# Summing W's first four units in two halves, with the output weight's second half converted behind W's beginning

## The chip, the cores and the metric

One core of a Trainium2 chip runs the whole program. The metric is the device time in microseconds (us), the median of several runs. Five engines work beside one another, each through its own instructions in program order: TensorE (PE, the matmuls), VectorE (DVE), ScalarE (ACT), GpSimd (POOL) and SyncE (SP, which here only issues loads). They wait for one another by semaphores alone.

## What is computed

The reference chains three layers. The first is a decaying linear attention over 2 batches of 8 heads, 768 positions and 64 columns in blocks. Its output x, 1536 tokens by 512, goes through a gated layer without an activation between its last two weights, and the result goes through a mixture of 8 experts that takes the best expert of each token:

```python
a, b = x @ w1, x @ w2
h = (a * b) @ w3            # w3: 1024 x 1024
y = h @ w_out               # w_out: 1024 x 512
logits = y @ w_gate         # 8 experts; the largest one is taken
```

## The kernel before

Since nothing stands between w3 and w_out, the kernel multiplies weights first: W = w3 @ [w_out, w_out @ w_gate], 1024 by 520. Its last 8 columns give the logits. Three products stand for each fp32 product (mm3, L293 to L297): high part by low part, high by high, low by high, where a high part is a cast to the fast fp32 format and a low part is the rest.

**Stages.** First attention (to about 59 us), then W (to about 108 us), then the gate units and the product with W, then the experts. Attention runs eight iterations, one for each batch and pair of heads. Iteration `it` has two parts. `part1(it)` forms the scores on TensorE (L391), masks them on VectorE into `at` (L400), and sums decayed keys by values (L413, the kv product) into states (L421). `part2(it - 1)` follows it: it multiplies `at` by the values (L439) and queries by states (L453), in two halves, and after each half ScalarE casts the result to `xth` (L462) and VectorE forms the rest `xtl` (L463). The last `part2` stands behind the loop. Decayed keys `kd` for the next iteration come from ScalarE at the end of each iteration (`decay_keys`, L362).

**Chunks and ticks.** In the shadow of all this, weights are converted. w1, w2, w3 and w_out come as 64-bit numbers, in chunks of 512 per partition (512 KB, `Item64`). w_out has two items of four chunks (`wo_it`), w3 four (`w3_it`), and a list fixes the order of all chunks. A tick (`Feed.tick`) takes every chunk under way one stage further and then starts the next one, and ticks are written into the program at fixed places (`TICKS` in attention, `run_bg` elsewhere). The stages of a chunk, a tick each:

1. its start: ScalarE turns the raw data into two parts (L132, into a PSUM bank called raw, and L133);
2. VectorE joins them into an fp32 `t` (the pair L135, L138), which frees the raw bank and the chunk's staging slot;
3. ScalarE casts `t` to the high part (L142), and GpSimd forms the low part (L143).

The w_out chunks go on, two at a time (`u_block`):

4. TensorE transposes two chunks' `t` into two banks (L219), ScalarE copies them to `wt` (L222, a pair of copies);
5. TensorE multiplies `wt` by w_gate (L227), and after the fourth chunk ScalarE copies the result to `up` (L236).

`u_ready` sums `up` (L241) and VectorE puts the eight gate columns behind the item's 512 (L250, L251). `feed.need(item)` ticks until an item is done.

**What sets the order.** Each engine keeps the order of the program. Loads are issued on SP in program order too: `LOADS` says how many chunks are loaded in each iteration beside the next queries, keys (`qk`) and keys, values (`kv`). The first four chunks have a place of their own, the others take four staging slots in turn, so chunk n waits for stage 2 of chunk n - 4. PSUM has seven banks for general use (`bank()`); the bank that came free first, in program order, is the next one given out, and whoever writes to it waits for its last reader.

**W.** Sixteen units, one for each block of 128 rows (`fb`) and half of the columns (256 or 264). A unit sums 24 matmuls over the eight blocks `jb` of w_out's rows (`w_steps`), four of the first item and four of the second; then ScalarE casts the sum to `wxh` (L520), VectorE forms `wxl` (L521), and one or two ticks follow (`NW`). Units go by quarters of w3: four units for each item.

Of the kernel before, what the change touches and what calls it, by code (L numbers as in the profile page):

```python
# [32 lines left out]
NW = (2, 1, 1, 1, 1, 1, 1, 1)  # L33
HOOK = 6
OVER = 7
LOADS = (1, 2, 2, 2, 2, 2, 2, 0)
TICKS = ((0, 0, 0, 0), (0, 0, 0, 1)) + ((1, 0, 0, 1),) * 6 + ((0, 0, 1, 0),)
XBW = 265


# [1 line left out]
def tile_moe_chain(ctx, tc, cap, qk, kv, w12, w3i, woi, wgi, e1i, e2i, c32, c16, zero, out):  # L42
# [8 lines left out]
    def pool(name, bufs=1, **kw):  # L51
        return tc.tile_pool(name=name, bufs=bufs, reuse_waits="tile", **kw)
# [3 lines left out]
    ring = ctx.enter_context(pool("ring"))  # L56
# [7 lines left out]
    def bank():  # L64
        return ps.tile([P, 512], F32, tag="b", name="bank")
# [3 lines left out]
    slots = {"ring": ring}  # L69
# [134 lines left out]
    feed = Feed()  # L204

    def run_bg(n=1):
        for _ in range(n):
            feed.tick()
# [29 lines left out]
    def u_ready(it):  # L238
        u = bank()
        for jb in range(4):  # L240
            nc.tensor.matmul(  # L241
                u[:, jb * NE : (jb + 1) * NE],
                it.up[:, jb * P : (jb + 1) * P],
                gsum,
                start=True,
                stop=True,
            )
        it.us = us = u[:, 0 : 4 * NE].rearrange("p (j e) -> p j e", e=NE)
        uh, ul = it.view(it.hi)[:, :, 512:520], it.view(it.lo)[:, :, 512:520]
        nc.vector.tensor_copy(uh, us)  # L250
        nc.vector.tensor_tensor(ul, us, uh.bitcast(F32), op=ALU.subtract)  # L251

    wo_it = [Item64(woi[j], "ring", "01"[j], 520, u_block) for j in range(2)]
    w3_it = [Item64(w3i[j], "ring", "23"[j]) for j in range(2)]
    w3_it += [Item64(w3i[j], "p0", "w3") for j in range(2, 4)]
    w12_it = [Item64(w12[j], "ring", "2301"[j]) for j in range(4)]
    for n in range(2):
# [7 lines left out]
    for w, e, j in turn[0:2] + turn[4:5] + turn[2:4] + turn[5:]:  # L265
        tag = min(until, key=until.get)
        it = Item((e1i, e2i)[w][e, j], "p3g" if tag == "x" else "ring", tag)
# [26 lines left out]
    def mm3(acc, wh, wl, rh, rl, first, last):  # L294
        nc.tensor.matmul(acc, wh, rl, start=first, stop=False)  # L295
        nc.tensor.matmul(acc, wh, rh, start=False, stop=False)  # L296
        nc.tensor.matmul(acc, wl, rh, start=False, stop=last)  # L297


    with pool("att", 2, side="right") as ap, pool("att1", side="right") as a1:  # L300
# [56 lines left out]
        def decay_keys(it):  # L357
            if it == 8:
                return
            kds[it] = ap.tile([P, NC - 1, P], F32, tag="kd", name="kd", bufs=1)  # L360
            for h in range(2):
                nc.scalar.activation(  # L362
                    kds[it][:, :, h * 64 : h * 64 + 64],
                    loads[it][1][:, 0, 0 : NC - 1, h * 64 : h * 64 + 64],
                    AF.Copy,
                    scale=dmask[:, (it // 2 * 2 + h) % 4, P - 1 : P],
                )
# [63 lines left out]
        def part2(it, ticks, qs, at, st):  # L431
            pair, b = divmod(it, 2)
            tkv = loads[it][1]
            os = [bank(), bank()]
            for cc in range(NC):
                half, c = divmod(cc, 3)
                for h in range(2):
                    hs = slice(h * 64, h * 64 + 64)
                    nc.tensor.matmul(  # L439
                        os[half][hs, c * P : (c + 1) * P],  # L440
                        tkv[:, 1, cc, hs],
                        at[:, h, cc, :],
                        start=c == 0,
                        stop=cc == 0,
                        skip_group_check=True,
                    )
            for half, o in enumerate(os):
                for c in range(3):
                    cc = half * 3 + c
                    for h in range(2):  # L450
                        hs = slice(h * 64, h * 64 + 64)
                        if cc:
                            nc.tensor.matmul(  # L453
                                o[hs, c * P : (c + 1) * P],
                                st[hs, cc - 1, :],
                                qs[hs, cc, :],
                                start=False,
                                stop=True,
                                skip_group_check=True,
                            )  # L460
                xh, xl = xt[2 * b + half]
                nc.scalar.copy(xh[:, pair, :], o[:, 0:G])  # L462
                nc.vector.tensor_tensor(  # L463
                    xl[:, pair, :], o[:, 0:G], xh[:, pair, :].bitcast(F32), op=ALU.subtract
                )
                if half == 0:
                    run_bg(ticks[2])

        prev = None
        for it in range(8):  # L470
            cur = part1(it, TICKS[it])
            if prev is not None:
                part2(it - 1, TICKS[it], *prev)
            if it + 2 < 8:
                load_qkv(it + 2)
            prev = cur
            feed.load(LOADS[it])
            if it == 2:
                nc.scalar.dma_start(wg_sb, wgi)
            if TICKS[it][3]:  # L480
                feed.tick(mid=lambda: decay_keys(it + 1))
# [4 lines left out]
        feed.need(wo_it[0])  # L486
        part2(7, TICKS[8], *prev)
        run_bg(TICKS[8][3])
        feed.auto = True
        feed.need(*wo_it)  # L490
        woh = [it.view(it.hi) for it in wo_it]
        wol = [it.view(it.lo) for it in wo_it]


    wpool = late.enter_context(pool("wext", side="right"))
    wxh = wpool.tile([P, 8, 520], F32R, name="wxh")
    wxl = wpool.tile([P, 8, 520], F32R, name="wxl")
    with pool("p0", 2, side="right") as p0:
        slots["p0"] = p0
        enabled.update(w3_it + w12_it[:2])  # L500
        halves = (slice(0, 256), slice(256, 520))

        def w_steps(acc, fb, cs, jbs):
            item = w3_it[fb // 2]
            fs = slice(fb % 2 * P, (fb % 2 + 1) * P)
            lh = item.hi[:, 0:2048].rearrange("p (j f) -> p j f", f=256)
            ll = item.lo[:, 0:2048].rearrange("p (j f) -> p j f", f=256)
            for jb in jbs:
                mm3(
                    acc,  # L510
                    lh[:, jb, fs],
                    ll[:, jb, fs],
                    woh[jb // 4][:, jb % 4, cs],
                    wol[jb // 4][:, jb % 4, cs],
                    jb == 0,
                    jb == 7,
                )

        def w_out(acc, fb, cs):
            nc.scalar.activation(wxh[:, fb, cs], acc, AF.Copy, scale=2.0**-16)  # L520
            nc.vector.scalar_tensor_tensor(  # L521
                wxl[:, fb, cs],
                acc,
                2.0**-16,
                wxh[:, fb, cs].bitcast(F32),
                op0=ALU.mult,
                op1=ALU.subtract,
            )
            run_bg(NW[fb])

        for i in range(4):
            units = [(fb, cs) for cs in halves for fb in (2 * i, 2 * i + 1)]
            feed.need(w3_it[i])
            for n, (fb, cs) in enumerate(units):
                acc = bank()[:, 0 : cs.stop - cs.start]
                w_steps(acc, fb, cs, range(8))
                if i + n == 0:
                    u_ready(wo_it[1])
                w_out(acc, fb, cs)

    gp = late.enter_context(pool("gt", 9, side="right"))
    p2 = late.enter_context(pool("p2", 2, side="right"))
# [28 lines left out]
    def x2_half(blk, cs, hooks={}):  # L571
        g, tb = divmod(blk, 3)
        ts = slice(tb * P, (tb + 1) * P)
        acc = bank()[:, 0 : cs.stop - cs.start]
        for fb in range(8):
            gh, gl = gts[g, fb]
            mm3(acc, gh[:, ts], gl[:, ts], wxh[:, fb, cs], wxl[:, fb, cs], fb == 0, fb == 7)
            if fb in hooks:
                hooks[fb]()
        return acc  # L580
# [161 lines left out]
    xd, accs = {}, {}  # L742
# [69 lines left out]
    acc = x2_half(NBLK - 1, slice(0, 256), {HOOK: lambda: dispatch(0, 1, apart=True)})  # L812
# [74 lines left out]
    for e in range(NE):  # L887
# [12 lines left out]
        for s in range(nmain):  # L900
            acc = bank()
            ss = slice(s * P, (s + 1) * P)
            for fb in range(8):
                it = e2_it[2 * e + fb // 4]
# [90 lines left out]
```

## Time and profile before

| what | value |
|---|---|
| median of 3 runs | 516.88 us |
| lowest and highest | 516.68 and 518.69 us |
| the profiled execution's own time | 516.84 us |
| its span, first to last instruction | 514.8 us |
| mean granted TensorE clock | 0.997 of full |
| TensorE busy | 498.6 us, 97% |
| VectorE, ScalarE busy | 264.9 and 242.9 us |

Busy times are of one profiled execution. A matmul's row is longer than the distance to the next row, since matmuls are pipelined: the pace is read from the starts. An instruction's idle time is that of its engine just before it, and what ended it is inferred from semaphores; where the engine named had long been done, it was another one.

### The profile page before, as it was taken

The page shows a single profiled execution, that of the slowest core. Times are in us where ns is not written, and L with a number is a line of the kernel's source. Part 1 is how long each engine was busy: PE and PEld are TensorE (multiplying, and loading weights), DVE is VectorE, ACT ScalarE, POOL GpSimd, SP SyncE. Part 2 cuts the span into 40 slices and gives each one's busy share as a digit, 9 for nine tenths or more (in the row PEclk, how much of TensorE's full clock was granted, in tenths as well). Part 3 has the DMA queues.
Part 4 walks back from the last instruction along what each step waited for, and adds up shares of the span by engine and source line. Part 5 has one row for each costly group of instructions (what it writes and reads, how often), then busy time and mean ns, then how long its engine had stood idle before and what let it go on. Part 6 is the DMA issues. An engine that isn't in the chain of part 4 may idle for free. (4 is left out here: it accounts for less than half of the span.)

```text
span 514.8 us, 9557 instructions
## 1 busy us (share of the span) xinstructions
PE 498.6 (97%) x3805; PEld 468.7 (91%) x3805; DVE 264.9 (51%) x576; ACT 242.9 (47%) x485; POOL 128.7 (25%) x124
## 2 busy tenths in 40 slices
PE   8999999999999999999999998899999999999993
PEld 4888999999999999999999998789989898989892
DVE  5998875668332223222332563468383746547420
ACT  2697997789311221122112424457464746546310
POOL 4365664545100000000020005405414040410101
PEclk9999999999999999999999999999999999999998
DMA  8999565557801000100010224486666666574200
GB/s 325 413 410 375 155 227 204 189 187 247 320 26 41 1 0 23 43 1 0 23 43 0 88 69 157 162 299 219 214 213 211 224 224 228 177 250 171 83 2 34
DMA packets 24529, 80.80 MB, mean 157 GB/s; under 512 B 3642, under 2 KB 5692, under 8 KB 24480
## 3 DMA queue, kind: packets, MB, share of 16 engines
q1 hardware_dynamic: 18976, 70.35, 38.4%
q0 software_dynamic: 3344, 7.85, 4.8%
q10 hardware_dynamic: 2160, 1.94, 1.1%
q8 instruction: 32, 0.52, 0.4%
q14 instruction: 17, 0.14, 0.1%
HBM read 74.84 MB, written 10.54 MB: 166 GB/s over the span
## 5 line engine op out<-in xcount | busy, mean ns | idle before, releaser
L97 DVE TENSOR_TENSOR wlo<-st,whi 128x512 fp32r<-128x512 f32 x128 | 82.0, 684 | 16.7 <-ACT whi L95 16.7
L295 PE MATMUL bank<-xtl,whi 128*128 128x384 f32 x256 | 87.1, 340 | 0.0
L297 PE MATMUL bank<-xth,wlo 128*128 128x384 f32 x256 | 86.4, 337 | 0.0
L296 PE MATMUL bank<-xth,whi 128*128 128x384 f32 x256 | 85.8, 335 | 0.0
L95 ACT CAST whi<-st 128x512 fp32r<-128x512 f32 x128 | 73.1, 621 | 16.2 <-PE bank L297 10.7
L787 PE MATMUL bank<-xdl,whi 128*128 128x256 f32 x256 | 72.6, 283 | 4.7 <-issue 2.5
L787 PE MATMUL bank<-xdh,whi 128*128 128x256 f32 x256 | 72.2, 282 | 0.0
L787 PE MATMUL bank<-xdh,wlo 128*128 128x256 f32 x256 | 72.1, 282 | 0.0
L143 POOL TENSOR_TENSOR wlo<-t,whi 128x512 fp32r<-128x512 f32 x40 | 51.9, 1298 | 52.1 <-ACT whi L142 46.5
L295 PE MATMUL bank<-wxl,gh 128*128 128x264 f32 (+1 forms) x192 | 55.9, 291 | 0.0
L296 PE MATMUL bank<-wxh,gh 128*128 128x264 f32 (+1 forms) x192 | 54.1, 282 | 0.0
L297 PE MATMUL bank<-wxh,gl 128*128 128x264 f32 (+1 forms) x192 | 54.1, 282 | 0.0
L787 PEld LDWEIGHTS bank<-xdl,whi 128*128 128x128 f32 x256 | 48.4, 189 | 5.6 <-issue 2.7
L564 DVE TENSOR_TENSOR a_sb<-bank,a_sb 128x384 f32<-128x384 f32 x32 | 17.8, 557 | 66.9 <-PE bank L297 66.3
L295 PE MATMUL bank<-wlo,hh 128*128 128x512 f32 x128 | 51.1, 399 | 0.0
L297 PE MATMUL bank<-whi,hl 128*128 128x512 f32 x128 | 50.4, 394 | 0.0
L718 POOL DMA_INDIRECT out_dram<-y,idx x16 | 16.6, 1038 | 134.2 <-ACT y L920 101.1
L296 PE MATMUL bank<-whi,hh 128*128 128x512 f32 x128 | 50.0, 391 | 0.0
L800 DVE SCALAR_TENSOR_TENSOR hl<-bank,hh 128x512 fp32r<-128x512 f32 x32 | 22.1, 690 | 53.3 <-ACT hh L799 45.5
L787 PEld LDWEIGHTS bank<-xdh,whi 128*128 128x128 f32 x256 | 48.3, 189 | 0.3
L787 PEld LDWEIGHTS bank<-xdh,wlo 128*128 128x128 f32 x256 | 48.4, 189 | 0.0
L295 PEld LDWEIGHTS bank<-xtl,whi 128*128 128x128 f32 x256 | 48.1, 188 | 0.0
(109 smaller groups left out, 1006.1 us busy)
## 6 DMA issues: line engine op xcount, KB each, us to landing
st<-e1i SPq DMA_DIRECT2D x32, 512.0 KB
st<-e2i SPq DMA_DIRECT2D x32, 512.0 KB
st<-w3i SPq DMA_DIRECT2D x16, 512.0 KB
st<-w SPq DMA_DIRECT2D x16, 512.0 KB
tqk<-qk SPq DMA_DIRECT2D x8, 768.0 KB
tkv<-kv SPq DMA_DIRECT2D x8, 768.0 KB
st<-woi SPq DMA_DIRECT2D x8, 512.0 KB
out_dram<-zero SPq DMA_DIRECT2D x1, 3072.0 KB
```

The source lines that it names most:

```text
L95: nc.scalar.copy(h, s)
L97: nc.vector.tensor_tensor(lo, s, h.bitcast(F32), op=ALU.subtract)
L143: nc.gpsimd.tensor_tensor(lo, t, h.bitcast(F32), op=ALU.subtract)
L295: nc.tensor.matmul(acc, wh, rl, start=first, stop=False)
L296: nc.tensor.matmul(acc, wh, rh, start=False, stop=False)
L297: nc.tensor.matmul(acc, wl, rh, start=False, stop=last)
L564: nc.vector.tensor_tensor(a_sb, acc, a_sb, op=ALU.mult)
L718: nc.gpsimd.indirect_dma_start(out=out, out_offset=bass.IndirectOffsetOnAxis(ap=idx[:, col : col + 1], axis=0), in_=src, in_offset=None, b ...
L787: nc.tensor.matmul(o, w[:, k, :], x[:, k, :], start=m == 0 and k == 2 and x is xl, stop=m == 1 and k == 1 and w is lo, skip_group_check=True,)
L800: nc.vector.scalar_tensor_tensor(hl, acc, 0.0, hh.bitcast(F32), op0=ALU.max, op1=ALU.subtract)
```

## The change

The order of items becomes w_out's first, w3's first, w_out's second, w3's second, by building the two lists in turn. Attention has a tick less, in the middle of iteration 3, and its second iteration loads one chunk in place of two. The wait for both w_out items ahead of W is gone. W's first four units are summed over `jb` 0 to 3 one after the other, each into a bank of its own that stays open, with a tick behind each; then `need` asks for w_out's second item, and the four are summed over `jb` 4 to 7 and go out as before. The gate sum of the second item (`u_ready`) stays behind the first finished unit. The other twelve units are as they were. `wt` for chunks that come in W is taken from W's pool.

```diff
--- before.py
+++ after.py
@@ -33,8 +33,9 @@
 NW = (2, 1, 1, 1, 1, 1, 1, 1)
 HOOK = 6
 OVER = 7
-LOADS = (1, 2, 2, 2, 2, 2, 2, 0)
-TICKS = ((0, 0, 0, 0), (0, 0, 0, 1)) + ((1, 0, 0, 1),) * 6 + ((0, 0, 1, 0),)
+LOADS = (1, 1, 2, 2, 2, 2, 2, 0)
+TICKS = ((0, 0, 0, 0), (0, 0, 0, 1), (1, 0, 0, 1), (0, 0, 0, 1)) + ((1, 0, 0, 1),) * 4
+TICKS += ((0, 0, 1, 0),)
 XBW = 265
 
 
@@ -250,8 +251,10 @@
         nc.vector.tensor_copy(uh, us)
         nc.vector.tensor_tensor(ul, us, uh.bitcast(F32), op=ALU.subtract)
 
-    wo_it = [Item64(woi[j], "ring", "01"[j], 520, u_block) for j in range(2)]
-    w3_it = [Item64(w3i[j], "ring", "23"[j]) for j in range(2)]
+    wo_it, w3_it = [], []
+    for j in range(2):
+        wo_it.append(Item64(woi[j], "ring", "01"[j], 520, u_block))
+        w3_it.append(Item64(w3i[j], "ring", "23"[j]))
     w3_it += [Item64(w3i[j], "p0", "w3") for j in range(2, 4)]
     w12_it = [Item64(w12[j], "ring", "2301"[j]) for j in range(4)]
     for n in range(2):
@@ -487,16 +490,13 @@
         part2(7, TICKS[8], *prev)
         run_bg(TICKS[8][3])
         feed.auto = True
-        feed.need(*wo_it)
-        woh = [it.view(it.hi) for it in wo_it]
-        wol = [it.view(it.lo) for it in wo_it]
 
 
     wpool = late.enter_context(pool("wext", side="right"))
     wxh = wpool.tile([P, 8, 520], F32R, name="wxh")
     wxl = wpool.tile([P, 8, 520], F32R, name="wxl")
     with pool("p0", 2, side="right") as p0:
-        slots["p0"] = p0
+        slots["p0"] = slots["att"] = p0
         enabled.update(w3_it + w12_it[:2])
         halves = (slice(0, 256), slice(256, 520))
 
@@ -510,8 +510,8 @@
                     acc,
                     lh[:, jb, fs],
                     ll[:, jb, fs],
-                    woh[jb // 4][:, jb % 4, cs],
-                    wol[jb // 4][:, jb % 4, cs],
+                    wo_it[jb // 4].view(wo_it[jb // 4].hi)[:, jb % 4, cs],
+                    wo_it[jb // 4].view(wo_it[jb // 4].lo)[:, jb % 4, cs],
                     jb == 0,
                     jb == 7,
                 )
@@ -531,12 +531,21 @@
         for i in range(4):
             units = [(fb, cs) for cs in halves for fb in (2 * i, 2 * i + 1)]
             feed.need(w3_it[i])
-            for n, (fb, cs) in enumerate(units):
-                acc = bank()[:, 0 : cs.stop - cs.start]
-                w_steps(acc, fb, cs, range(8))
-                if i + n == 0:
-                    u_ready(wo_it[1])
-                w_out(acc, fb, cs)
+            parts = (range(4), range(4, 8)) if i == 0 else (range(8),)
+            accs = [None] * 4
+            for jbs in parts:
+                if jbs[0] == 4:
+                    feed.need(wo_it[1])
+                for n, (fb, cs) in enumerate(units):
+                    if jbs[0] == 0:
+                        accs[n] = bank()[:, 0 : cs.stop - cs.start]
+                    w_steps(accs[n], fb, cs, jbs)
+                    if jbs[-1] < 7:
+                        run_bg(1)
+                        continue
+                    if i + n == 0:
+                        u_ready(wo_it[1])
+                    w_out(accs[n], fb, cs)
 
     gp = late.enter_context(pool("gt", 9, side="right"))
     p2 = late.enter_context(pool("p2", 2, side="right"))
```

## Rows read from the trace of the kernel before

**Rows 1.** The page: span; busy us and share of each engine.

```profile
span 514.8 us, 9557 instructions
PE 498.6 (97%) x3805; PEld 468.7 (91%) x3805; DVE 264.9 (51%) x576; ACT 242.9 (47%) x485; POOL 128.7 (25%) x124
```

**Rows 2.** Waits of TensorE, 0 to 315 us: who, for whom, total, times, longest.

```profile
PE bank L325 <- DVE warm L319: 1.2, 1, 1.2
PE bank L413 <- DVE t L138: 0.9, 1, 0.9
PE bank L391 <- DVE xtl L463: 0.8, 1, 0.8
PE bank L413 <- ACT kd L362: 0.3, 1, 0.3
```

**Rows 3.** Table of stretches: length, busy (instructions) per engine, clock, DMA share, GB/s.

```profile
24.21:48.70 24.49, 24.48 (x383) 21.08 (x383) 23.01 (x44) 20.96 (x41) 16.27 (x13) 1.00 1.02 408
...
59.30:71.84 12.54, 12.54 (x107) 12.54 (x106) 9.61 (x18) 10.31 (x20) 6.53 (x5) 1.00 0.59 190
```

**Rows 4.** TensorE in attention: start, length, line, tiles [idle before, by whom ended].

```profile
23.72 1.10 PE L413 MATMUL bank<-tkv,kd 128*64 128x64 f32 x19 [0.94 <-DVE t L138]
...
27.46 1.09 PE L219 MATMUL bank<-c_sb,t 128*128 128x128 f32 x8
28.48 1.61 PE L391 MATMUL bank<-tqk 64*128 64x128 f32 x24
30.02 0.64 PE L227 MATMUL u<-wt,wg_sb 128*32 128x256 f32 x8
30.59 1.07 PE L413 MATMUL bank<-tkv,kd 128*64 128x64 f32 x19
...
42.06 0.96 PE L241 MATMUL bank<-c_sb,up 128*128 128x8 f32 x8
42.95 1.85 PE L391 MATMUL bank<-tqk 64*128 64x128 f32 x24
...
50.93 1.60 PE L391 MATMUL bank<-tqk 64*128 64x128 f32 x22 [0.75 <-DVE xtl L463]
```

**Rows 5.** ScalarE in attention, in order of time.

```profile
23.02 1.01 ACT L362 ACTIVATE kd<-tkv,dmask 128x320 f32<-128x320 f32 x2 [0.75 <-DMA tkv<-kv]
24.21 0.67 ACT L132 ACTIVATE bank<-st 128x512 f32<-128x512 f32 x1 [0.18 <-DMA st<-woi]
...
48.70 0.65 ACT L132 ACTIVATE bank<-st 128x512 f32<-128x512 f32 x1 [2.49 <-DMA st<-w3i]
...
50.56 1.08 ACT L222 COPY wt<-bank 128x512 f32<-128x512 f32 x2
51.52 0.64 ACT L142 CAST whi<-t 128x512 fp32r<-128x512 f32 x1
52.03 1.03 ACT L362 ACTIVATE kd<-tkv,dmask 128x320 f32<-128x320 f32 x2
```

**Rows 6.** VectorE: one chunk's pair and the masked scores behind it.

```profile
51.26 0.69 DVE L135 SCALAR_TENSOR_TENSOR bank<-bank,st 128x512 int32<-128x512 int32 x1
52.05 0.69 DVE L138 SCALAR_TENSOR_TENSOR t<-st,bank 128x512 int32<-128x512 int32 x1
52.66 1.94 DVE L400 TENSOR_TENSOR at<-bank,dmask 128x384 f32<-128x384 f32 x4
```

**Rows 7.** TensorE: first matmul of W's first and of its fifth unit.

```profile
59.30 0.39 PE L295 MATMUL bank<-wlo,whi 128*128 128x256 f32 x1
...
71.79 0.28 PE L295 MATMUL bank<-wlo,whi 128*128 128x256 f32 x1
```

**Rows 8.** ScalarE in W: two casts of a finished unit, two ticks between them.

```profile
69.08 0.39 ACT L520 ACTIVATE wxh<-bank 128x264 fp32r<-128x264 f32 x1
...
73.24 0.37 ACT L520 ACTIVATE wxh<-bank 128x264 fp32r<-128x264 f32 x1
```

## The prediction

> **What bounds the kernel now.** The page comes first: TensorE is busy 498.6 of the 514.8 us span [rows 1], so only its idle time can be won before the last output leaves. The waits of TensorE, read next, hold four rows for the stretch up to 315 us [rows 2]: 1.2 us before the first warm-up product and 0.3 us early on, which the change doesn't reach, 0.9 us in attention's iteration 3 and 0.8 us in iteration 7. W and all gate units show none. The most that the change can give back there is 0.94 + 0.75 = 1.69 us [rows 4]. The table of stretches tells what holds attention: from 24.21 to 48.70 us VectorE is busy 23.01 of 24.49 us and the DMA engines the whole time at 408 GB/s [rows 3].
>
> The time I sum against is the profiled execution's own 516.84 us (span 514.8 and 2.04 around it), 0.04 under the median of the three runs, 516.88.
>
> **What moves.** Chunks are numbered in their new order: 0 to 3 the output weight's first half, 4 to 7 W3's first quarter, 8 to 11 the output weight's second half, 12 on the next W3 quarters. One tick leaves iteration 3, so 13 chunks start before W in place of 14. Four ticks stand behind the four first sums, so ten ticks lie in W's first four units in place of six. The second half's transposes for chunks 8 and 9 fall between the two halves of the last part2, their product after W's first sum, and chunks 10 and 11 have transposes and product in W. So TensorE work leaves attention: one transposing step, 28.48 - 27.46 = 1.02, and two products of 30.59 - 30.02 = 0.57 each [rows 4], 2.16 us. All of it comes back in W, so this alone is worth 0. The matmuls of W are as many as before. A tick less relieves ScalarE of some 1.66 us and VectorE of 52.66 - 51.26 = 1.40 [rows 6]. (1.66 is L142 at 52.03 - 51.52 = 0.51 [rows 5] and two L132-like visits at an estimated 0.57, row lengths less their overlap.) One pair of wt copies, 51.52 - 50.56 = 0.96 [rows 5], and one gate copy, an estimated 0.46, leave as well.
>
> **Loads.** SP's order has one 512 KB chunk less ahead of attention's later inputs. By ScalarE's waits chunk 2 landed at 24.21 and the first chunk behind the last kv at 48.70 [rows 5]; between them lie eight inputs of 768 KB and seven chunks, 9.96 MB in 24.49 us, 407 GB/s, so 1.29 us for a chunk. The chunk that iteration 6 waits for then lands at 47.41, and every qk and kv from iteration 4 on 1.29 us earlier. The kv of iteration 3 stays where it is, with the 0.94 us gap that it makes: its decayed keys wait for it until 23.02 [rows 5]. On SP each weight load waits for its staging slot alone, that is for the VectorE pair of the chunk four before. Chunk 12 is loaded by its own tick now, but SP comes to it at 51.6, when chunk 8's slot is free; ScalarE wants it at 59.6, and 1.29 us of transfer fit in between.
>
> **Attention's end.** I carry the four engines on in program order, with starts taken from the rows' distances, and banks handed out first freed first.
> - Iteration 4: the scores run from 27.46, 1.02 earlier, to 29.0. The transposes of chunks 0 and 1 now stand behind them, and one of their two banks is the raw bank of chunk 2, whose VectorE pair stands behind the residual of iteration 2 and ends at 29.95. The kv product's bank is the second score bank, read by VectorE until 29.95 + 0.97 = 30.9. Together TensorE idles 0.82.
> - Iteration 5: the same two waits, VectorE being busy from 28.6 on, 0.26.
> - Its end: the gate sum of the first half (L241) stands directly behind the product whose copy it reads, and the copy behind the last xt cast: 0.73 before its own 0.89 (42.95 - 42.06 [rows 4]). Before, a whole part2 lay between product and sum. What waits behind it on TensorE are the scores of iteration 6.
> - Iteration 7: chunk 8's conversion (47.41 and two ScalarE visits), the residual of iteration 5 and chunk 8's VectorE pair follow each other to 51.6. Its raw bank is the one of the kv product, while the scores end at 50.6: 0.95. The old 0.75 at 50.18 is gone.
>
> Sum: 0.82 + 0.26 + 0.73 + 0.95 - 0.75 = 2.0 us of new idle. W begins at 59.30 - 2.16 + 2.0 = 59.15, next to nothing earlier. The trace doesn't show these waits; their bounds are -0.75 (none comes, the old one goes) and +3.0 (each of the four places costs as much as the longest such row, 0.94, less the old 0.75). I take 2.0, since VectorE's chain fixes three of them.
>
> **W's beginning.** The first four sums need no fifth bank, but three of the seven banks now serve all raw chunks, transposes and the gate sum. With first freed first, the fifth unit's bank is the one that chunk 18 had, in the tick after the second finished unit. Unhindered TensorE would reach this unit at 59.15 + 12.49 (71.79 - 59.30 [rows 7]) + 2.16 = 73.8. ScalarE's way there: the last xt cast stands behind the wt copies of chunks 8 and 9 and chunk 12's start, and ends by 61.17; a tick to 62.83; the second transposes end at 63.36; wt copies and a tick to 65.98; gate copy and a tick to 68.10; a tick to 69.76; the first wxh cast (0.28) and two ticks to 73.65, with 0.28 lost to chunk 16's VectorE pair. VectorE then does the second wxl and chunk 18's pair, to 75.95. So TensorE waits 75.95 - 73.8 = 2.15. Behind the waiting matmul stand the twelve later units and the gate units, which is all of TensorE's work; ScalarE and VectorE wait for none of it, having lag to work off. The nearest row for this pace is the same pattern before, two ticks between wxh at 69.08 and at 73.24, 4.16 us [rows 8], against my 3.89; in that stretch ScalarE was already busy 10.31 of 12.54 us with six ticks [rows 3]. Bounds: 0, if the bank comes from elsewhere, and 3.8, if the pace of that row holds throughout (0.3) and chunk 8 lands no earlier than 48.70 (1.3). I take 2.15, being nearest to the row. Afterwards a unit gives ScalarE 1.94 us of work in some 2.83 us of TensorE (24 matmuls at 0.118, from the rows' starts), so it recovers, and the next banks come in time. The three chunks it is ahead in the end save nothing, as W had no wait.
>
> In W before, each unit's sum sits in another bank and TensorE shows no wait [rows 2]. The Trainium skill (Perfetto Trace Analysis, Optimizing Tensor Performance, Matmuls) wants independent groups to rotate through banks so that emptying one overlaps the next one's matmuls. The change gives that up for eight steps. By that rule alone one emptying would lie bare, about twice the wxh row's 0.39 us [rows 8], and the time would be 516.84 + 2.0 + 0.8 = 519.6.
>
> Sum: unit 5 starts at 75.95 against 71.79, +4.16, and nothing behind it can absorb that, since TensorE goes on without a wait [rows 2]: 516.84 + 4.16 = 521.0.
>
> **Rivals.**
> - *No bank wait in W* (0.25). For it: TensorE had no wait there before. Against it: ten ticks in place of six where ScalarE was at 82%. Then only attention's 2.0 remains: 518.8.
> - *Attention shortens by all that leaves it* (0.10), the other side. The place is iteration 7: with chunk 8 at 47.41 and a wt pair and a tick gone, VectorE could take chunk 8's pair before the scores end. The price is the 0.75 us wait at 50.93 that vanishes with nothing new: 516.84 - 0.75 = 516.1. It decides at W's start: at 56.4 (59.30 - 2.16 - 0.75) or before it holds. Against it: VectorE has at most 1.5 us of slack in 24 us [rows 3].
> - *The wait in W comes again* (0.15): ScalarE lags by more than I have, so units 6 and 7 also find their banks in use by late chunks. One more wait of about 2.4 us, the distance of one tick with its unit at the 4.16 pace: 523.4.
> - That the change doesn't do what it says is not likely: its order is fixed by the loops.
>
> **How the numbers follow.** Forecast 521.0, chance 0.50, its own range 519.6 to 522.4. The range takes in the first and the third rival, 517.2 to 523.8; what lies under it is the second one and some more, 0.12, and 0.06 lies over it. A measurement of this kernel can tell about 0.5%, 2.6 us, from no change: 514.3 to 519.4 is the same. Faster by more needs gains that no TensorE wait offers: 0.03, out of the second rival. Within: 0.22 of the first rival, 0.07 of the second and 0.05 of the forecast's lower edge, 0.34. Slower: 0.45 of the forecast, 0.03 of the first rival and the third one's 0.15, 0.63.
>
> **What would show it.** In the waits of TensorE: a wait of 2 to 2.5 us at the first matmul of the fifth W unit, ended by VectorE (L138); waits of 0.7 before L241 in iteration 5 and of about 1 before L413 in iterations 4 and 7; the 0.75 before L391 gone. ScalarE's first load wait shorter and at 47.4. First W matmul near 59.1. The forecast is wrong if W starts before 58, if the fifth unit starts without a wait, or if a stretch behind W changes its length.

## The result, and the profile after

The changed kernel takes 524.19 us (median of 4 runs, 523.31 to 526.23) against 517.30 us beside it: 1.0132 times the time before, 95% interval 1.0108 to 1.0157. It is slower, as forecast, but the time lies 0.4 us above the top of the forecast range, 523.8. The profiled execution took 524.52 us, 7.68 us more than that of before.

The page after, span and busy time (lines of the changed kernel are one to nine higher than before):

```profile
span 522.5 us, 9565 instructions
PE 501.7 (96%) x3805; PEld 471.3 (90%) x3805; DVE 265.2 (51%) x576; ACT 243.5 (47%) x485; POOL 127.6 (24%) x124
```

TensorE is busy 3.1 us more than in [rows 1] with the same 3805 matmuls: some of them ran slower. Its waits up to 322 us, as in [rows 2]:

```profile
PE bank L298 <- DVE t L139: 2.8, 1, 2.8
PE bank L416 <- ACT kd L365: 2.2, 3, 0.9
PE bank L328 <- DVE warm L322: 1.2, 1, 1.2
PE bank L242 <- ACT up L237: 0.7, 1, 0.7
PE bank L220 <- DVE t L139: 0.6, 1, 0.6
PE bank L394 <- DMA tqk<-qk: 0.2, 1, 0.2
```

The first one is the bank wait at W's fifth unit, ended by VectorE's conversion; the 0.7 stands before the gate sum, the 0.6 before the transposes of iteration 4; the 0.75 before the scores of iteration 7 is gone. TensorE at W's first unit, its fifth and the first gate unit, to be held against [rows 7]:

```profile
59.09 0.39 PE L298 MATMUL bank<-wlo,whi 128*128 128x256 f32 x1
...
76.91 0.35 PE L298 MATMUL bank<-wlo,whi 128*128 128x256 f32 x1 [2.75 <-DVE t L139]
...
113.03 0.34 PE L298 MATMUL bank<-xtl,whi 128*128 128x384 f32 x1
```

W begins 0.21 us earlier, its fifth unit 5.12 us later, the gate units (106.33 before) 6.70 us later. So 1.58 us more went lost in W's last twelve units, where TensorE shows no wait at all. The table of stretches tells where (columns as in [rows 3]):

```profile
74.00:77.00 3.00, 0.24 (x3) 0.12 (x2) 1.89 (x4) 3.00 (x8) 1.65 (x2) 1.00 0.70 209
77.00:78.30 1.30, 1.30 (x12) 1.30 (x13) 1.20 (x3) 1.17 (x3) 0.81 (x1) 1.00 0.84 299
78.30:81.70 3.40, 3.40 (x19) 3.40 (x18) 2.68 (x5) 3.40 (x7) 2.15 (x3) 0.50 0.80 247
81.70:90.00 8.30, 8.30 (x70) 8.30 (x70) 5.96 (x11) 6.77 (x14) 4.85 (x4) 1.00 0.76 256
334.29:337.70 3.41, 3.02 (x14) 3.02 (x15) 0.94 (x2) 0.18 (x2) 1.50 (x2) 0.50 0.15 44
```

Behind the bank wait the granted clock falls to 0.50, the lower of its two levels, for 3.41 us. The same happens at 334.29 at a wait in the experts' beginning, which was there before without a fall. The wait before, the stretch behind it, and the wait after:

```profile
328.12 0.39 PE L787 MATMUL bank<-xdl,whi 128*128 128x256 f32 x1 [2.51 <-issue]
```

```profile
328.00:330.00 2.00, 1.88 (x15) 1.88 (x16) 0.66 (x2) 0.15 (x1) 1.28 (x1) 1.00 0.22 66
```

```profile
334.68 0.58 PE L796 MATMUL bank<-xdl,whi 128*128 128x256 f32 x1 [2.45 <-issue]
```

The second fall accounts for the remaining 0.98 us (7.68 - 6.70). TensorE's lag behind the kernel before stays at 6.70 us up to 295 us, rises over the matmuls of that stretch to 7.85 at 337.62 (329.77 before) and is 7.70 at 476 us.

### The profile page after: what moved, and what is told of

It is laid out like the page before. It is cut to its first block, busy times and chain, and to the rows that moved or that the text cites. A ratio compares the mean times of both kernels' runs of the same rounds, so it can differ in the third digit from the quotient of the medians.

```text
span 522.5 us, 9565 instructions
## 1 busy us (share of the span) xinstructions
PE 501.7 (96%) x3805; PEld 471.3 (90%) x3805; DVE 265.2 (51%) x576; ACT 243.5 (47%) x485; POOL 127.6 (24%) x124
## 3 DMA queue, kind: packets, MB, share of 16 engines
q0 software_dynamic: 3344, 7.85, 4.7%
## 5 line engine op out<-in xcount | busy, mean ns | idle before, releaser
L300 PEld LDWEIGHTS bank<-xth,wlo 128*128 128x128 f32 x256 | 48.1, 188 | 0.0
```

## Experiments

Runs fell on chips on which the kernel before takes about 513.3 us and on others where it takes about 517.5. Every time is given over the kernel before on the same chip; on one chip, that of the second filled kernel, the kernel before took from 514.04 to 517.76. In the profiles from the first kind the wait of 2.5 us in the experts' beginning is missing, and the one 12 us ahead of it, 1.1 to 1.3 us on the others, is 0.33 us (the second filled kernel's profile has 2.36 and 0.33).

| kernel | median, us over before | ratio, 95% interval | W begins | W's length |
|---|---|---|---|---|
| changed, again | +5.90 | 1.0130 [1.0087, 1.0173] | 58.68 | 54.10 |
| its wait filled | +5.52 | 1.0089 [1.0057, 1.0120] | 59.25 | 52.83 |
| one tick for block 0 | +2.67 | 1.0049 [1.0035, 1.0063] | 59.11 | 49.44 |
| new order, W unsplit | +5.85 | 1.0108 [1.0075, 1.0140] | 64.58 | 47.05 |
| W split alone, ten ticks | +6.07 | 1.0111 [1.0076, 1.0146] | 59.16 | 52.53 |
| the same, wait filled | +5.07 | 1.0101 [1.0081, 1.0121] | 59.31 | 51.72 |
| split alone, six ticks | +2.09 | 1.0048 [1.0033, 1.0063] | 59.11 | 49.08 |
| split alone, eight ticks | +0.66 | 1.0010 [1.0000, 1.0021] | 59.26 | 47.55 |
| one tick, gate sum late | +2.21 | 1.0046 [1.0029, 1.0062] | 59.16 | 49.45 |
| one tick, old ticks and loads | +4.46 | 1.0091 [1.0074, 1.0108] | 60.53 | 48.80 |
| one tick, chunk 8 early | +1.61 | 1.0032 [1.0020, 1.0045] | 58.58 | 49.44 |
| before, chunk 9 early | -1.22 | 0.9974 [0.9963, 0.9985] | 58.47 | 47.04 |

W's length is from its first matmul to the first gate matmul, 47.03 in the profile of before. Edits are given against the changed kernel, or against the kernel before where the text says so.

### Is it the clock?

```diff
+                    if (i, n) == (1, 0):
+                        fill = psi.tile([P, 512], F32, tag="i", name="fill")
+                        for r in range(22):
+                            nc.tensor.matmul(
+                                fill[:, 0:256],
+                                w3_it[0].hi[:, 0:P],
+                                wo_it[0].view(wo_it[0].hi)[:, 0, 0:256],
+                                start=True,
+                                stop=True,
+                            )
```

> The changed kernel with 22 extra matmuls (operands of W's first unit, 256 columns, into the bank of the gate sums) put ahead of W's fifth unit. They take away no wait: the fifth unit's bank still comes when VectorE has read chunk 18's raw data. Theory (the wait of 2.75 us lets the granted clock fall, and 3.4 us at half clock follow): the fifth unit starts at 76.9 as before within 0.3, the clock stays at 1.00 up to 90 us, W ends about 1.7 us earlier than in the changed kernel, near 522.5 us in all (less by another 1 if the fall at 334 us goes too). Rival (the slow matmuls behind the wait come from what the other engines do there, or from the bank order): the clock falls at 78 us all the same and the time is 524 or, by the added matmuls, more.

TensorE with the fill, and the stretches behind it:

```profile
74.16 2.79 PE L543 MATMUL fill<-whi 128*128 128x256 f32 x22
77.45 0.36 PE L298 MATMUL bank<-wlo,whi 128*128 128x256 f32 x1 [0.50 <-DVE t L139]
```

```profile
78.30:81.70 3.40, 3.40 (x31) 3.40 (x31) 2.52 (x6) 3.26 (x7) 2.36 (x2) 1.00 0.72 198
81.70:90.00 8.30, 8.30 (x72) 8.30 (x70) 6.66 (x13) 7.73 (x17) 5.22 (x4) 1.00 0.75 253
```

In the same 3.40 us there are 31 matmuls in place of 19, at the full clock, with the other engines as busy. W's last twelve units take 34.63 us (112.08 - 77.45), before 34.54, in the changed kernel 36.12. The fifth unit starts at 77.45, 0.5 us later than in the changed kernel and outside the 0.3 I allowed, so only 1.1 of the 1.5 us show in W's length, and on its own the median can't tell this from the changed kernel. The changed kernel, run again:

> The changed kernel unchanged, beside the others on one chip. On the chip of the four experiments so far the wait of 2.5 us in the experts' beginning was only 0.33 us, so no second fall of the clock is expected there: 6.6 us over the kernel before (2.2 of moved work, 2.8 of bank wait, 1.7 of half clock, 0.2 less in attention, 0.1 else). If the clock had no part in it, 5 us over.

It came out at +5.90, between the two figures, and its interval holds both. In the profile the wait was 2.99 us, the clock fell at its end, and no second fall came. But the four executions are not alike. A fall of 3.41 us takes 0.003 off the mean granted clock of an execution, and the last 3 us or more, at 0.50 in every profile, take as much. The profiled one, 519.64 us, has 0.992. Two others have 0.997 and 0.996, which leaves no room for a fall, and take 518.30 and 518.88 us, +4.94 and +5.52; the last has 0.990 and takes 522.54. So in half of these executions no fall came; how long the wait was in them is not known.

As a fall kept away once might be chance, a second pair: the kernel split alone with ten ticks, of the section after next, whose wait is longer, with 27 extra matmuls.

> The kernel before with W's first four units split and their four more ticks (ten in all), and 27 extra matmuls ahead of the fifth unit, in whose place TensorE waited 3.67 us without them. Theory (the wait makes the clock fall, in each case where it is long enough and TensorE does nothing in it): the fifth unit starts 16.6 us behind W's first matmul as without the fill, within 0.4, the clock stays at 1.00, and W's last twelve units take 34.6 us instead of the 35.9 without the fill. Rival (the filled case before kept its clock by chance, as one gap of 2.5 us in the experts keeps it and another does not): the clock falls again and the twelve units take 35.9 us or more.

The clock stayed at 1.00 in W, and the twelve units took 34.63 us (111.03 - 76.40) in place of 35.88. The fifth unit starts 17.09 us behind W's first matmul, just outside what I allowed (16.6 within 0.4). In all three profiles with an unfilled wait of 2.75 us or more in W the clock fell; in both filled ones it did not.

### Is it the bank?

```diff
-NW = (2, 1, 1, 1, 1, 1, 1, 1)
+NW = (1, 1, 1, 1, 1, 1, 1, 1)
```

> The changed kernel with one tick instead of two behind W's units of row block 0, so eight ticks in W's first four units instead of ten. Theory (the fifth unit waits for the bank of a late chunk): the bank now handed out is that of the second finished unit, free near 72.6 us, so the wait of 2.75 us is gone, the clock does not fall at 78 us, and the time is 4.5 us less, near 519.7 us; what is left against the kernel before is TensorE's work moved out of attention, some 2 us, and perhaps the fall near 334 us, 1 us. Rival (the fifth unit waits for the conversion of W3's second quarter, not for a bank): the wait stays or grows and the time stays near 524 us.

TensorE's waits from 20 to 100 us:

```profile
PE bank L416 <- ACT kd L365: 1.6, 2, 0.9
PE bank L242 <- ACT up L237: 0.7, 1, 0.7
PE bank L220 <- DVE t L139: 0.6, 1, 0.6
PE bank L394 <- DVE xtl L466: 0.2, 1, 0.2
```

TensorE at the fifth unit:

```profile
74.02 0.28 PE L298 MATMUL bank<-wlo,whi 128*128 128x256 f32 x1
```

The wait in W is gone, though W3's conversion is two ticks further back, so it was not W3's second quarter that the fifth unit waited for; that leaves the bank, as the wait's row says. W is 4.5 to 4.7 us shorter, and the first four units take 14.91 us (74.02 - 59.11) against 12.49: 2.42 us, the moved work with no wait around it.

### The split or the order?

Against the kernel before, only the loop of W is taken from the change (ten ticks in its first four units):

> The kernel before with W's first four units summed in two halves and a tick behind each first half, nothing else: attention, its order, ticks and loads are those of before. Theory (the bank wait and the clock are the split's, by its four more ticks on three free banks): W begins at 59.3 us, the fifth unit's bank is chunk 19's, free near 74.1 us, while TensorE is there at 71.8: a wait of 2.3 us, then half clock for 3.4 us: 516.9 + 2.3 + 1.7 = 520.9 us. Rival (the split is free, the loss comes from the new order with the output weight's copies and transposes in W): no wait, 516.9 us.

```profile
PE bank L295 <- ACT wxh L520: 3.7, 1, 3.7
PE bank L413 <- DVE t L138: 0.9, 1, 0.9
PE bank L391 <- DVE xtl L463: 0.7, 1, 0.7
```

The wait came and is longer than worked out, 3.67 us for 2.3, and the time is 2 us above the expectation. The list names the cast of a finished unit, not a late chunk. The rows say otherwise:

```profile
74.97 0.69 DVE L138 SCALAR_TENSOR_TENSOR t<-st,bank 128x512 int32<-128x512 int32 x1
75.33 0.37 ACT L520 ACTIVATE wxh<-bank 128x264 fp32r<-128x264 f32 x1
75.74 0.43 DVE L521 SCALAR_TENSOR_TENSOR wxl<-bank,wxh 128x264 fp32r<-128x264 f32 x1
75.81 0.55 PE L295 MATMUL bank<-wlo,whi 128*128 128x256 f32 x1 [3.67 <-ACT wxh L520]
```

The late chunk's pair ends at 75.66 and the cast at 75.70, but VectorE reads that unit's bank until 76.17, behind the matmul's start. So it can't be the bank waited for, and the late chunk's can. In the changed kernel pair and cast end at 76.76 and 76.80, as close together, and there the list names VectorE. Why the wait is 1.4 us longer than worked out was not followed up. Without the four ticks:

```diff
-                        run_bg(1)
                         continue
```

> The kernel before with W's first four units summed in two halves but no tick behind a first half, so six ticks in these units as before. Theory (splitting the sums costs nothing by itself; the four more ticks do): no wait in W longer than 0.3 us, W takes 47.0 us and the time is within 0.3 us of the kernel before. Rival (holding four banks open is enough to stop TensorE): a wait at the fifth unit of 1 us or more, and 1 to 4 us over the kernel before.

Here my theory fell. TensorE, in W:

```profile
73.58 0.36 PE L295 MATMUL bank<-wlo,whi 128*128 128x256 f32 x1 [1.80 <-ACT wxh L520]
```

With as many ticks as before the four finished units come within 6.8 us (73.58 - 1.80, less the second halves' start at 64.97), and ScalarE has their casts and six ticks to do in that time. Here too VectorE's pair (to 73.44) and a cast (to 73.48) end together ahead of the matmul. Four sums held open cost 1.8 us even without more ticks. The rule of the Trainium skill that the prediction weighed (Perfetto Trace Analysis, Optimizing Tensor Performance, Matmuls), that independent sums should rotate through banks, bears on this; the wait of 1.80 us agrees with it, but doesn't show that the open sums alone make it. The eight-tick version asks whether spreading the ticks heals it:

> The kernel before with W's first four units summed in two halves, a tick behind each first half and one behind each finished unit: eight ticks in these units, four of them early. Theory (with six ticks behind the finished units, ScalarE has too much to do in the short time of the second halves; with the ticks spread it keeps up): no wait in W over 0.3 us, W begins at 59.2 us and takes 47.0 to 47.3 us, the time is within 0.4 us of the kernel before, and what the changed kernel with one tick has over it, 2.4 us, is then the new order's. Rival (four open banks stop TensorE however the ticks lie): a wait of 1 us or more at the fifth unit, 1 to 3 us over the kernel before.

No wait of 0.1 us or more is left in W. W takes 47.55 us, 0.25 more than I allowed, and the time is 0.66 us over before where I allowed 0.4 (its interval runs from no change to 0.2%). So the split costs little with four ticks early and four late. What makes the wait is not the open sums alone but the ticks behind the finished units: with six of them there TensorE waits, with or without four early ones, and with four it doesn't. What the changed kernel with one tick has over this one, 2.67 less 0.66, is 2.0 us; it goes with the new order, its ticks and its loads. The order alone, with W as before:

```diff
         feed.auto = True
+        feed.need(*wo_it)
...
-            parts = (range(4), range(4, 8)) if i == 0 else (range(8),)
+            parts = (range(8),)
```

> The changed kernel with W unsplit: the new order of chunks, ticks and loads, but the wait for both halves of the output weight ahead of W as in the kernel before, and its first four units whole. Theory: attention still ends near 59.1 us, since its waits do not depend on W; three ticks then stand ahead of W, in which TensorE has 2.2 us of work and waits about 3 us for transposes, copies and conversions; W begins near 64.4 us, only six ticks lie in its first four units and its fifth unit does not wait; 522 us, or 523.7 if the clock falls in the gap. Rival (the new order alone is a gain and the split spoils it): W begins before 61 us and the time is under 518 us.

W begins at 64.58, worked out were 64.4, and the time is 5.85 us over for 5.1, so the new order alone is no gain either. The gap ahead of W was 2.47 us long, and the clock stayed at 1.00 behind it:

```profile
PE u L228 <- ACT wt L223: 2.5, 1, 2.5
```

### What holds attention's end?

The kernels of this section but the last are the changed one with one tick behind W's units of row block 0. First the gate sum, an iteration later:

```diff
             feed.load(LOADS[it])
+            if wo_it[0].done == 4 and not hasattr(wo_it[0], "us"):
+                u_ready(wo_it[0])
...
-            if wo_it[0].done == 4 and not hasattr(wo_it[0], "us"):
-                u_ready(wo_it[0])
```

> The changed kernel with one tick behind W's units of row block 0 and the gate sum of the output weight's first half moved one iteration later, behind the next part2, so that it stands far behind the copy it reads. Theory (attention's end hangs on chunk 8, whose load lands near 47.4 us): the wait of 0.7 us before the gate sum goes, the wait of 0.9 us in iteration 7 grows by as much, W begins at 59.1 us as before, and the time is that with one tick alone, 2.6 us over the kernel before. Rival (each of these waits counts by itself): W begins at 58.4 us and the time is 1.9 us over the kernel before.

```profile
PE bank L416 <- ACT kd L365: 1.6, 2, 0.9
PE bank L416 <- issue: 0.8, 1, 0.8
PE bank L220 <- DVE t L139: 0.6, 1, 0.6
```

```profile
44.28 0.80 PE L416 MATMUL bank<-tkv,kd 128*64 128x64 f32 x20 [0.79 <-ACT kd L365]
```

The 0.7 before the gate sum is gone, and 0.79 has come before the kv product of iteration 6, not of 7 as I had it (there it is 0.77, the second row of the list, for 0.91). W begins at 59.16. Removing this one wait of TensorE moves nothing. With the old ticks and loads (LOADS and TICKS as before the change):

> The changed kernel with the ticks and loads of the kernel before (14 chunks started before W) and one tick behind W's units of row block 0. Theory: attention is held by VectorE and the load that iteration 6 waits for, here chunk 9 as in the kernel before, so the 1.6 us of TensorE work that leaves it turns mostly into waits; W begins between 58.5 and 59.5 us, no wait in W over 0.5 us, and the time is 1 to 2 us over the kernel before. Rival (the new order pays once no tick is taken out): W begins near 57 us and the time is 0.5 to 1 us under the kernel before.

Both expectations missed: W begins at 60.53, and the kernel is 4.5 us over. Given the new order, the tick and the load that were taken out are worth 1.4 us of attention (60.53 - 59.11). W itself is 0.64 us shorter than with one tick alone. The profiled execution took 516.28 us at a mean clock of 0.997, the other three 517.67 to 518.05 at 0.991, so a part of the 4.5 us may be falls of the clock; that was not followed up. Last, the loads:

```diff
-LOADS = (1, 1, 2, 2, 2, 2, 2, 0)
+LOADS = (1, 1, 2, 2, 2, 1, 2, 0)
...
+            if it == 4:
+                feed.load(1)
```

> The changed kernel with one tick behind W's units of row block 0, and chunk 8 loaded at the end of iteration 4, ahead of the last queries, keys and values. Theory (attention's end hangs on chunk 8's load): it lands near 43.6 us instead of 47.4, ScalarE's wait of 1.5 us for it goes, W begins 0.8 to 1.2 us earlier, near 58.1 us, and the time is 1.4 to 1.8 us over the kernel before. Rival (VectorE's queue in program order holds it, not the load): W begins at 59.1 us, 2.4 us over the kernel before.

ScalarE in iteration 6, in the changed kernel and then here:

```profile
47.58 0.65 ACT L133 ACTIVATE bank<-st 128x512 f32<-128x512 f32 x1 [1.54 <-DMA st<-woi]
```

```profile
45.58 0.66 ACT L133 ACTIVATE bank<-st 128x512 f32<-128x512 f32 x1
46.16 0.70 ACT L134 ACTIVATE st<-st 128x512 int32<-128x512 uint16 x1
47.99 0.48 ACT L465 CAST xth<-bank 128x384 fp32r<-128x384 f32 x1 [1.13 <-PE bank L456]
```

It no longer waits for chunk 8, and W begins 0.53 us earlier, against the 0.8 to 1.2 I expected. The rest is held elsewhere: a wait of 1.01 us before the kv product of iteration 7 stays. That product starts at 51.17, 0.09 us behind the end of chunk 8's pair on VectorE (50.39 + 0.69), which stands behind the residual there. So the rival, VectorE's order, holds the other half. The same edit on the kernel before (there it is chunk 9, and LOADS[5] goes from 2 to 1):

> The kernel before with chunk 9 loaded at the end of iteration 4, ahead of the last queries, keys and values, nothing else. Theory (in the kernel before, too, the one wait that can go is made by a load): ScalarE's wait of 2.5 us at 48.7 goes, with it TensorE's 0.75 us before the scores of iteration 7, W begins near 58.5 us and the time is 0.7 us less than before, 0.15%. Rival (the wait is VectorE's, whose queue is full): W begins at 59.3 us, no change.

TensorE there in iteration 7:

```profile
48.77 1.09 PE L219 MATMUL bank<-c_sb,t 128*128 128x128 f32 x8
49.80 1.61 PE L391 MATMUL bank<-tqk 64*128 64x128 f32 x24
51.34 0.64 PE L227 MATMUL u<-wt,wg_sb 128*32 128x256 f32 x8
```

The wait of 0.75 us [rows 4] is gone, W begins at 58.47, and the kernel takes 0.9974 of the time before (0.9963 to 0.9985): faster than both, by moving one load. W's beginning shows 0.83 of the 1.22 us. Where the rest comes from is not shown; the falls of the clock differ between executions (last section).

## Why the prediction was wrong

- **Attention's end was right in number, by luck in part.** 59.09 against 59.15. The waits came where they were put: 0.59 and 0.1 in iteration 4 (0.82 forecast), 0.1 in iteration 5 (0.26), 0.71 at the gate sum (0.73), 0.91 in iteration 7 (0.95), and chunk 8 was there at 47.58 (47.41). With the old 0.75 gone that is 1.66 us and not 2.0; a wait of 0.23 us for queries in iteration 3 and other small ones, not forecast, made up for it. The list puts the 0.91 down to decayed keys, but these were done at 51.01:

  ```profile
  49.98 1.03 ACT L365 ACTIVATE kd<-tkv,dmask 128x320 f32<-128x320 f32 x2
  50.90 0.69 DVE L139 SCALAR_TENSOR_TENSOR t<-st,bank 128x512 int32<-128x512 int32 x1
  51.69 0.80 PE L416 MATMUL bank<-tkv,kd 128*64 128x64 f32 x20 [0.91 <-ACT kd L365]
  ```

  Chunk 8's pair on VectorE ends at 51.59, 0.10 us ahead of the product; 51.6 was forecast, and its bank as the cause. That the waits can be summed one by one is not borne out: with the gate sum's taken away another came.
- **The moved work was right and a little small.** 2.16 forecast; 2.42 from the kernel without a bank wait, 2.58 in the changed kernel (76.91 - 2.75 - 59.09 - 12.49).
- **The bank wait was right in place and cause, and small.** 2.15 forecast, 2.75 measured; the bank came at 76.91 and not at 75.95. ScalarE behind the fifth tick of W shows part of it:

  ```profile
  72.37 0.62 ACT L143 CAST whi<-t 128x512 fp32r<-128x512 f32 x1 [0.23 <-DVE t L139]
  73.41 0.65 ACT L133 ACTIVATE bank<-st 128x512 f32<-128x512 f32 x1 [0.42 <-DMA st<-w3i]
  ```

  Chunk 18's load, asked for when chunk 14's slot came free, landed 0.42 us late. I had taken every load of W as on time. Another 0.34 us comes earlier: the second copies to `wt` start at 63.70, behind transposes that I had at 63.36. The rest of the 0.96 was not traced.
- **The step that failed is the sum: "+4.16, and nothing behind it can absorb that, since TensorE goes on without a wait".** It goes on without a wait, but not at its pace. The sum held no term for the clock. The fall behind the bank wait cost 1.58 us in W (36.12 less 34.54, of which the filled kernel gives 1.49 back), the second one 0.98. With the fifth unit 0.96 us later than worked out (5.12 for 4.16), 0.96 + 1.58 + 0.98 = 3.52, which is 524.52 - 521.0. The prediction's own sign of being wrong, a stretch behind W that changes its length, came. The trace of before shows the clock whole behind a wait of 2.51 us; the prediction doesn't weigh whether that holds for another wait. The Trainium skill (TensorE: Matmul & The Clock Gate, The HAM clock gate) calls the lower level the default, which activity lifts: the traces agree that idle TensorE can bring it back, 0.50 for 3.41 us, but it did not each time.
- **The range** rested on the waits alone, 523.8 at its top with the bank wait twice. It did not come twice; the clock took its place.
- **The rivals.** No bank wait: no. Attention shorter by all that leaves it: no, it is 0.21 us shorter. The rule on rotating banks deserved more than its 0.8 us: the split with six ticks waits 1.8, though with eight, four of them early, it doesn't wait.

## What to carry to other kernels

A wait on an engine that is busy all the time need not be paid once: price what can follow it too, here half as much again where the clock falls. When sums are held open, count what is left of the banks and who else takes them in turn, and spread the background work over the time in which they are open. And before moving work out of a stage, see what its last wait hangs on; in the kernel before it was the place of one load in a queue. A row that names who ended a wait is to be checked against that one's end: twice here it named an instruction that was done or could not have freed the bank.

## What the runs showed that I had not expected

The length of a gap alone does not tell whether the clock falls behind it. Waits of 2.36, 2.43, 2.45 and 2.48 us at the experts' beginning had 3.41 us at 0.50 begin at their end or behind it (split and filled, chunk 8 early, changed, chunk 9 early), while 2.51 and 2.52 us there (before, split with eight ticks) and 2.47 us ahead of W (unsplit) had none. All three unfilled waits from 2.75 us on had it, in the profiles; of the four executions of the changed kernel run again two had no fall, by their mean clock. Times that differ by about a microsecond from one execution to the next, whatever is changed ahead, fit this: with chunk 9 early, six executions at a mean clock of 0.996 or 0.997 took 515.42 to 516.18 us, and six at 0.991 to 0.994 took 517.04 to 517.47. Of these one was profiled and has the fall; that the other five have it is not shown. The profiles from the chips where the kernel before takes 513.3 us don't have the wait of 2.5 us; why, no run here tells.
